# Attention and mixture-of-experts on one core: product 1's base sums are read from PSUM by VectorE, and the next w2's scale comes from a read of its own, a step earlier

## The chip, the cores and the metric

The kernel runs on one core of a Trainium2 chip. The metric is the device time of one execution in microseconds (us). The engines are TensorE (PE in the profile; its weight loads are PEld), VectorE (DVE), ScalarE (ACT), GpSimd (POOL) and SyncE (SP), which here issues nearly all DMA transfers, in one order.

## What is computed

The reference, cut to its core. Attention has 4 batches, 8 heads, 768 positions and 64 numbers a head; its output is the input of a layer with 8 experts, in which every expert works on all 3072 rows:

```python
scores = np.where(mask, scale * np.matmul(q, k.transpose(0, 1, 3, 2)), -1e9)
attn = softmax(scores)
x = np.matmul(attn, v)                      # as 3072 x 512
P = balance(np.exp(x @ w_gate))             # 3072 x 8, eight rounds of normalising
for e in range(8):
    h = np.maximum(x @ w1[e], 0.0)          # 512 -> 1024
    ye = h @ w2[e]                          # 1024 -> 512
    out += P[:, e:e+1] * ye
```

## The kernel before

**Arithmetic.** All numbers are float32 on the outside. For TensorE each operand is scaled by a power of two and split into two float16 parts, and three of the four products of parts are added. The matrix products of the experts are made with seven products instead of eight for each 2 x 2 block of sub-matrices, so there are sums of sub-matrices of x, w1, w2 and h to make (GpSimd, VectorE), scales to find (eight passes of `magnitude`, L122, on ScalarE, then `whole`, `spread` and `power` in `scale_steps`), and splits (`queue_split`: ScalarE writes the high part, L1281, VectorE the low part, L1285).

**Stages.** Attention takes the first 440 us or so. Then 32 steps follow, i = 4e + b for expert e and batch b. The main loop weaves two generators: `outputs(i)`, which calls `stage2` (the second layer: h times w2, 42 units of 12 matmuls at L1801 into banks `py`, each followed by an eviction into `acc` by VectorE, L1823), and `products(i+1)`, which calls `stage1` (the first layer for the next step: for each of four column groups seven products of 12 matmuls at L1664 into banks `p`, with VectorE's `comb`, L1513, then a high part of h on ScalarE, L1680, and a low part on VectorE, L1685 and L1691, or GpSimd, L1691). At the end of a column group `add` makes four sums on GpSimd, `s` (L1750) and three more (L1303); they wait for ScalarE's `a` (L1747), and parts of h wait for them.

**The fine products.** From the third expert on, two of the seven products (0 and 1) are themselves made with seven sub-products of 6 matmuls (L1552). `fine(i+1)` does that, one step ahead, in 14 pieces that `products` puts between the products of `stage1`; the table `BETWEEN` tells how many pieces come after which product of which column group. Product 0 uses the banks fx, fy, fz, product 1 the banks gx, gy, gz. The banks of `p`, f and g are four in all (`ps_h`). The first sub-product of each is a base that is added to what three of the four quarters become. For product 1 this is

```python
nc.scalar.activation(t0, two(bx), AF.Copy, scale=HDOWN)      # L1609, from gx
nc.gpsimd.tensor_tensor(out=at_(sums_, f, t), in0=t0, in1=at_(pair, f, t), op=ALU.add)
```

the second line (L1612) three times; the fourth quarter is made by `comb` from gx after its second sub-product. `xpf` holds the parts of x that the sub-products need; it is loaded again (L1437) for product 1 and for the next step's product 0, after its last reader.

**Weights.** One buffer `r` of 2 MB (tag "r") takes the raw weights in turn: w1 of the next expert is loaded in an expert's second step (`b == LB1`), w2 of the next expert in the last step, after the second of its seven products, both by L205 on SyncE. A buffer with the tag "s3" holds w1's third sum, or w2's first sum `t1`. What has to be done with a weight is not written where it runs but handed to `Slots`: three queues with estimated costs, which `tick` empties as the estimated busy times of VectorE, ScalarE and GpSimd allow. `need(key)` runs all that is left of a key. Work of some keys is also held back to its place by an ordering edge (`not_earlier`). For w2 before the change the order in the queue is: eight passes of the scale, `whole`, `spread` (a TensorE transpose into `all_w`, L135), `power`, then the sums (`queue_sum`, L1296) and splits of `split_w2`. The last scheduling is the compiler's, which orders every engine by its own estimate.

Of the kernel before, what the change touches and what calls it, by code (L numbers as in the profile page):

```python
# [9 lines left out]
F32 = mybir.dt.float32  # L10
# [10 lines left out]
P = 128  # L21
# [35 lines left out]
def tile_sparse_attention_moe(  # L57
# [153 lines left out]
        open_w(which, e)  # L211
        load_part(which, e, 0, 1)

    def scale_steps(which, e, vector=nc.vector, scalar=nc.scalar):
        flat = wr[which].rearrange("p c f -> p (c f)")
        n = 8
        w = KD * FF // n
        m = small.tile([P, n], F32, tag="mxw", name=f"mx_w{which}_{e}")
        a = small.tile([P, 1], F32, tag="maw", name=f"ma_w{which}_{e}")
        s = small.tile([P, 1], F32, tag=f"sw{which}", name=f"sw{which}_{e}")  # L220
        inv = small.tile([P, 1], F32, tag=f"iw{which}", name=f"iw{which}_{e}")
        wr["s", which], wr["i", which, e] = s, inv

        def part(k):
            magnitude(scalar, m[:, k : k + 1], flat[:, k * w : (k + 1) * w])

        def whole():
            vector.tensor_reduce(out=a, in_=m, axis=AX.X, op=ALU.max)

        def spread():  # L230
            wr["all", which] = spread_bound(a, spread_bank[0](f"all_w{which}_{e}"))

        def power():
            vector.tensor_reduce(out=a, in_=wr["all", which], axis=AX.X, op=ALU.max)
            vector.tensor_scalar(a, a, TINY, HUGE, ALU.max, ALU.min)
            ai = a.bitcast(I32)
            vector.tensor_scalar(ai, ai, 0x7F800000, None, ALU.bitwise_and)
# [965 lines left out]
    class Slots:  # L1203
# [13 lines left out]
        def run(self, queue, n):  # L1217
            fn, key, _, costs, _ = queue.pop(n)
            self.charge(costs)
            self.last[id(queue)] = self.now  # L1220
            if key[0] in ("scale", "w1", "w2", "late", "balance", "fine_x"):
                not_earlier(fn)
            else:
                fn()
# [4 lines left out]
                for x, c, lead in zip(self.busy, costs, LEADS)  # L1229
            )  # L1230

        def tick(self, pe, dve, act=0.0, turn=1.0, pool=0.0):
            self.now += turn
            self.pe += pe
            self.busy = [max(x, self.pe - lag) for x, lag in zip(self.busy, LAGS)]
            self.charge((dve, act, pool))
            n, held = 0, set()
            while n < len(self.urgent):
                _, key, ready, costs, _ = self.urgent[n]
                if key not in held and ready <= self.now and self.fits(costs):  # L1240
                    self.run(self.urgent, n)
                    n, held = 0, set()
                    continue
                held.add(key)
                if key[0][0] == "sum":
                    held.update((("h", key[1], p),) + key[1:] for p in (2, 4, 5, 6))
                n += 1
            for queue in (self.lazy, self.calm):
                while queue and self.due(queue):
                    self.run(queue, 0)  # L1250
# [18 lines left out]
    def scale_w(which, e):  # L1269
        parts, whole, spread, power = scale_steps(which, e, Pinned.vector, Pinned.scalar)  # L1270
        key = ("scale", which, e)
        for k, part in enumerate(parts):
            slots.add(part, key, 8 if k == 0 else 1, True, act=0.65)
        slots.add(whole, key, 1, True, dve=0.1)
        slots.add(spread, key, 1, True, gap=5)
        slots.add(power, key, 1, True, dve=0.8, gap=2)

    def queue_split(dst, src, key, delay=1):
        s = wr["s", 1 if key[0] == "w1" else 2]
# [78 lines left out]
    def split_w2(e, r):  # L1358
        h = KF // 2
        m = {  # L1360
            (j, k): r[:, j * h : (j + 1) * h, k * DH : (k + 1) * DH]
            for j in range(2) for k in range(2)
        }
        t1 = raw.tile([P, h, DH], F32, tag="s3", name=f"t1_{e}") if e else wr["t1"]

        def one(p, src):
            queue_split(w2p[p], src, ("w2", e, p))

        def sums():
            if e:  # L1370
                one(1, m[1, 0])
                queue_sum(t1, m[0, 1], m[0, 0], ("scale", 2, e))
                queue_sum(m[0, 1], m[0, 1], m[1, 1], ("scale", 2, e))

        def first():
            if e:
                one(0, m[0, 0])
                queue_sum(m[0, 0], m[1, 1], t1, ("w2", e, 5))
                queue_sum(m[1, 0], m[1, 0], m[0, 0], ("w2", e, 3))

        def second():
            one(6, m[0, 1])
            if e:
                one(5, m[0, 0])

        return [
            sums,
            first,
            second,
            lambda: (one(4, t1), one(3, m[1, 0]), one(2, m[1, 1])),  # L1390
        ]

    def balance():
# [125 lines left out]
    def fine(i, used=None):  # L1519
# [47 lines left out]
        def fresh(nm):  # L1567
            return two(upool.tile([P, TH], F32, tag="u", name=f"{nm}_{i}"))

        def tick(n, m, k=0.0):  # L1570
            slots.tick(0.495, 0.55 * n, 0.5 * m, 0.5, k)

        product = pieces(0)
        bx, t0 = bank_("fx"), fresh("t0")
# [28 lines left out]
        tick(1, 0)  # L1603
        yield

        product1 = pieces(1)
        bx, t0 = bank_("gx"), fresh("s0")
        product1(0, bx, True)
        nc.scalar.activation(t0, two(bx), AF.Copy, scale=HDOWN)  # L1609

        def base(f, t):
            nc.gpsimd.tensor_tensor(  # L1612
                out=at_(sums_, f, t), in0=t0, in1=at_(pair, f, t), op=ALU.add
            )

        base(1, 0)
        base(1, 1)
        tick(0, 1, 1.9)
        yield
        product(2, bz, False)  # L1620
        comb(t5, two(bz), t5)
        last(0)
        base(0, 1)
        tick(1, 0, 0.95)
        yield
        product1(1, bx, False)
        comb(at_(sums_, 0, 0), two(bx), at_(pair, 0, 0))
# [19 lines left out]
        yield  # L1647

    BETWEEN = {
        (1, 4): 1, (1, 2): 1, (2, 5): 1, (2, 6): 1, (2, 3): 1, (2, 4): 2, (2, 2): 2,  # L1650
        (3, 5): 1, (3, 6): 1, (3, 3): 1, (3, 4): 1, (3, 2): 1,
    }

    def stage1(i, qi, used=None):
# [238 lines left out]
    def outputs(i):  # L1893
        e, b = divmod(i, B)
        last = b == B - 1 and e + 1 < NE
        for n, p in enumerate(ORDER2):
            yield from stage2(i, p)
            if p == 4 and e + 1 < NE:
                move_acc(b, 1, True)
            if p == 4 and B <= i + 1 < NI:  # L1900
                move_acc((b + 1) % B, 1, False)
            if last and n == 1:
                for x in range(NP + 2):
                    slots.need(("w1", e + 1, x))
                load_w(2, e + 1)
                parts = split_w2(e + 1, wr[2])
                scale_w(2, e + 1)
                parts[0]()
                queue_weight(e + 1)
            elif last and n in (2, 4, 6):  # L1910
                parts[n // 2]()

    for i in range(NI):
# [8 lines left out]
            for p in range(NP):  # L1922
                slots.need(("w2", e, p))
        if b == LB1 and nxt:
            slots.need(("scale", 2, e + 1))
            load_w(1, e + 1)
            scale_w(1, e + 1)
            sum_w1(e + 1)
# [57 lines left out]
```

## Time and profile before

| | us |
|---|---|
| median of 3 runs | 2186.58 |
| lowest and highest run | 2185.72, 2186.83 |
| the profiled execution | 2186.69 |
| its span | 2184.8 |
| TensorE busy | 2124.3 (97%) |
| VectorE, ScalarE, GpSimd busy | 1662.7 (76%), 1241.0 (57%), 1623.0 (74%) |

The span is what the profiler saw between the first and the last instruction; 1.9 us of the execution lie around it. TensorE is busy for almost all of the span, at the full granted clock in all slices, so the time hangs on the 60.5 us in which it is not, and on whether they grow. In the rows below a bracket at the end of a line gives the idle time of the engine just before it and the instruction that ended it.

### The profile page before, as it was taken

To read this page: it belongs to the slowest core of one execution; us is meant where nothing else is said; L and a number is where in the kernel's file an instruction comes from. 1 tells how busy PE (TensorE), PEld (TensorE's weight loads), DVE (VectorE), ACT (ScalarE), POOL (GpSimd) and SP (SyncE) were. 2 spreads that over 40 slices of the span, in tenths; PEclk is the share of its full clock that TensorE was granted. 3 is DMA by queue.
4 is the path that set the end of the run, shared out by engine and by line. 5 is a ranking of instruction groups with operands and counts; after the bars stand their busy time and mean duration, and the time that the engine had idled before them with its cause. 6 is when DMAs were issued, how large, how long until landed. Compare 5 with 4: busy or idle time off the path is not lost.

```text
span 2184.8 us, 49326 instructions
## 1 busy us (share of the span) xinstructions
PE 2124.3 (97%) x19660; PEld 1644.7 (75%) x19660; DVE 1662.7 (76%) x3082; ACT 1241.0 (57%) x2386; POOL 1623.0 (74%) x1766
## 2 busy tenths in 40 slices
PE   6999999999999999999999999999999999999999
PEld 4777776677777777787878787877787777777787
DVE  8889998778877677767776777677777777777765
ACT  5888888766565556454555454445544555455442
POOL 5667778567668786878687868786878687868763
PEclk9999999999999999999999999999999999999999
DMA  6757795142244434443434343434343434343331
GB/s 171 191 128 172 172 213 142 51 156 102 97 151 162 144 111 162 146 140 117 162 131 155 124 162 124 162 124 162 123 162 124 162 124 162 123 162 131 124 102 66
DMA packets 220986, 305.73 MB, mean 140 GB/s; under 512 B 135228, under 2 KB 153684, under 8 KB 220756
## 3 DMA queue, kind: packets, MB, share of 16 engines
q1 hardware_dynamic: 220192, 302.56, 44.2%
q8 instruction: 153, 2.51, 0.5%
q14 instruction: 77, 0.63, 0.1%
q10 hardware_dynamic: 564, 0.03, 0.0%
HBM read 206.60 MB, written 64.49 MB: 124 GB/s over the span
## 4 chain that ended last, share of the span: by engine, by line
PE 71%; POOL 15%; DVE 7%; ACT 4%; issue 3%; DMA 1%; POOLq 0%; ACTq 0%; DVEq 0%
PE py L1801 31%; PE p L1664 23%; POOL r L1296 3%; POOL h L1691 3%; PE u L837 3%; DVE top L748 2%; POOL s L1750 2%; PE t L772 2%; PE t L775 2%; PE m L739 2%; PE m L742 2%; PE gy L1552 1%; PE fy L1552 1%; POOL r L1303 1%; POOL a L1303 1%
## 5 line engine op out<-in xcount | busy, mean ns | idle before, releaser
L1801 PEld LDWEIGHTS <-h 128*128 128x128 f16 x8064 | 786.1, 98 | 149.1 <-issue 14.3
L1801 PE MATMUL py<-w2p,h 128*128 128x256 f16 x4608 | 578.1, 273 | 8.6 <-DVE acc L1823 7.9
L1801 PE MATMUL py<-vault,h 128*128 128x256 f16 x3456 | 412.5, 273 | 2.9 <-DVE vault L1285 2.9
L1823 DVE SCALAR_TENSOR_TENSOR acc<-py,spare,acc 128x256 f32<-128x256 f32 (+1 forms) x588 | 301.8, 517 | 128.2 <-PE py L1801 120.8
L1750 POOL TENSOR_TENSOR s<-a,u 128x384 f32<-128x384 f32 x128 | 142.4, 1113 | 288.1 <-ACT a L1747 288.1
L1513 DVE SCALAR_TENSOR_TENSOR a<-p,a 128x384 f32<-128x384 f32 x384 | 211.5, 551 | 64.0 <-PE p L1664 62.0
L1691 POOL TENSOR_TENSOR h<-r,h 128x384 f16<-128x384 f32 x224 | 238.3, 1068 | 19.5 <-ACT h L1680 19.5
L1664 PEld LDWEIGHTS <-attic 128*128 128x128 f16 x1824 | 177.2, 98 | 94.0 <-issue 3.3
L1664 PE MATMUL p<-attic 128*128 128x384 f16 x1152 | 217.6, 326 | 0.6 <-DVE h L1685 0.4
L1680 ACT ACTIVATE h<-p 128x384 f16<-128x384 f32 x288 | 139.5, 484 | 136.7 <-DVE p L1513 136.3
L1685 DVE SCALAR_TENSOR_TENSOR h<-p,h 128x384 f16<-128x384 f32 x288 | 159.3, 553 | 62.7 <-ACT h L1680 29.4
L780 ACT ACTIVATE pe<-t,qk 128x768 int32<-128x768 f32 x192 | 172.4, 900 | 58.8 <-PE t L775 46.3
L748 DVE TENSOR_REDUCE top<-m 128x1 f32<-128x768 f32 x192 | 182.0, 950 | 29.8 <-PE m L742 28.7
L1664 PEld LDWEIGHTS <-w1p 128*128 128x128 f16 x1248 | 121.3, 98 | 63.8 <-issue 2.2
L1691 DVE TENSOR_TENSOR h<-s,h 128x384 f16<-128x384 f32 x128 | 106.3, 830 | 78.7 <-ACT h L1680 77.7
L1680 ACT ACTIVATE h<-s 128x384 f16<-128x384 f32 x128 | 66.6, 521 | 174.6 <-POOL s L1750 174.5
L1680 ACT ACTIVATE h<-r 128x384 f16<-128x384 f32 x224 | 114.3, 519 | 90.0 <-POOL r L1303 71.4
L1513 DVE SCALAR_TENSOR_TENSOR p<-p,u 128x384 f32<-128x384 f32 x256 | 142.7, 557 | 25.0 <-PE p L1664 23.4
L794 POOL TENSOR_SCALAR pl<-pe 128x768 f16<-128x768 uint16 x126 | 109.1, 867 | 68.1 <-ACT pe L780 67.4
L1303 POOL TENSOR_TENSOR r<-s,r 128x384 f32<-128x384 f32 x128 | 152.9, 1195 | 7.7
L1664 PEld LDWEIGHTS <-arena 128*128 128x128 f16 x1152 | 112.1, 98 | 61.2 <-issue 2.6
L837 PE MATMUL u<-vq,pl 128*128 128x65 f16 x1152 | 142.5, 193 | 1.0 <-POOL pl L794 0.6
(261 smaller groups left out, 4802.4 us busy)
## 6 DMA issues: line engine op xcount, KB each, us to landing
arena<-xd SPq DMA_DIRECT2D x126, 384.0 KB, 3.6
accd<-acc SPq DMA_DIRECT2D x56, 768.0 KB, 4.8
acc<-accd SPq DMA_DIRECT2D x56, 768.0 KB, 4.8
attic<-xd SPq DMA_DIRECT2D x96, 384.0 KB, 5.2
r<-in_moe_w_dram SPq DMA_DIRECT2D x14, 2048.0 KB, 9.2
xpf<-xfd SPq DMA_DIRECT2D x48, 384.0 KB, 4.9
arena<-in_q_dram SPq DMA_DIRECT2D x16, 384.0 KB, 4.1
arena<-in_k_dram SPq DMA_DIRECT2D x16, 384.0 KB, 4.5
```

The costliest lines, as they stand in the source:

```text
L748: nc.vector.tensor_reduce(out=tops[n][:, c : c + 1], in_=sc[:, :S], axis=AX.X, op=ALU.max)
L780: nc.scalar.activation(pe, sc[:, :S], AF.Exp, bias=EXP_SHIFT, scale=qk[n // 2][3])
L837: nc.tensor.matmul(uv[:, c, :n], lhsT=l[:, c * P : (c + 1) * P], rhs=w[:, h, kc, :n], start=(kc == 0 and c == 0 and m == 0), stop=(kc == N ...
L1303: nc.gpsimd.tensor_tensor(out=out, in0=x, in1=y, op=ALU.subtract)
L1513: nc.vector.scalar_tensor_tensor(out=t, in0=ps, scalar=HDOWN, in1=other, op0=ALU.mult, op1=ALU.add)
L1664: nc.tensor.matmul(ps, lhsT=w1ps[i // B][p][:, l, kc, fs], rhs=xp[p][:, r, kc], start=(kc == 0 and m == 0), stop=(kc == KH - 1 and m == 2),)
L1680: nc.scalar.activation(h[:, 0], src, AF.Relu if relu else AF.Copy)
L1685: nc.vector.scalar_tensor_tensor(out=h[:, 1], in0=src, scalar=0.0, in1=h[:, 0], op0=ALU.max, op1=ALU.subtract,)
L1691: eng.tensor_tensor(out=h[:, 1], in0=src, in1=h[:, 0], op=ALU.subtract)
L1750: nc.gpsimd.tensor_tensor(out=s1, in0=a1, in1=u3, op=ALU.add)
L1801: nc.tensor.matmul(py, lhsT=hs[i, p, kc][:, l, tsl], rhs=w2p[p][:, r, kc], start=(old is None and kc == 0 and m == 0), stop=(kc == KF // 2 ...
L1823: nc.vector.scalar_tensor_tensor(out=dst, in0=src, scalar=c, in1=dst, op0=ALU.mult, op1=ALU.add)
```

## The change

Two edits. In `fine`, the base of product 1 is no longer copied by ScalarE and added by GpSimd: VectorE makes the three base sums itself, each a `comb` with gx in PSUM as one operand. The piece that holds product 0's last sub-product now comes ahead of the piece with product 1's first, and `BETWEEN` puts one piece less after the sixth product of the third column group and one more after the first product of the fourth. `tick` loses its argument for GpSimd.

In the other, w2's scale is no longer taken from the 2 MB load itself. `early_scale(e+1)`, queued behind the last splits of w2 of expert e, that is in the first steps of expert e, fetches w2 of the next expert in four parts of 512 KB into a buffer of the tag "s3" and runs the eight passes on them, then `whole`, `spread` and `power`. All of it must be done before w1 of the next expert is loaded. When w2 is loaded for good, its sums and splits are queued without a scale ahead of them, under keys of their own, and the first split has a delay of 10.

```diff
+    def early_scale(e):
+        key = ("early", e)
+        steps = []
+
+        def fetch(k):
+            if k == 0:
+                t = raw.tile([P, KH, FH], F32, tag="s3", name=f"w2_{e}")
+                flat = t.rearrange("p k f -> p (k f)")
+                steps.extend(scale_steps(2, e, Pinned.vector, Pinned.scalar, flat))
+                steps.append(flat.rearrange("p (k f) -> p k f", f=DM))
+            nc.sync.dma_start(
+                out=steps[4],
+                in_=w2[e].rearrange("(c p) f -> p c f", p=P)[:, 2 * k : 2 * k + 2],
+            )
+
+        for k in range(KF // 2):
+            slots.add(lambda k=k: fetch(k), key, 1, True)
+            for n in range(2):
+                slots.add(
+                    lambda k=2 * k + n: steps[0][k](), key, 1, True, act=0.65,
+                    gap=0 if n else 5,
+                )
+        for n, (gap, dve) in enumerate(((0, 0.1), (5, 0.0), (2, 0.8))):
+            slots.add(lambda n=n: steps[1 + n](), key, 1, True, dve=dve, gap=gap)
...
         def sums():
             if e:
-                one(1, m[1, 0])
-                queue_sum(t1, m[0, 1], m[0, 0], ("scale", 2, e))
-                queue_sum(m[0, 1], m[0, 1], m[1, 1], ("scale", 2, e))
+                one(1, m[1, 0], 10)
+                queue_sum(t1, m[0, 1], m[0, 0], ("w2", e, 4))
+                queue_sum(m[0, 1], m[0, 1], m[1, 1], ("w2", e, 6))
...
+        def last():
+            one(4, t1)
+            one(3, m[1, 0])
+            one(2, m[1, 1])
+            if e + 1 < NE:
+                early_scale(e + 1)
...
-        product1 = pieces(1)
-        bx, t0 = bank_("gx"), fresh("s0")
-        product1(0, bx, True)
-        nc.scalar.activation(t0, two(bx), AF.Copy, scale=HDOWN)
-
-        def base(f, t):
-            nc.gpsimd.tensor_tensor(
-                out=at_(sums_, f, t), in0=t0, in1=at_(pair, f, t), op=ALU.add
-            )
-
-        base(1, 0)
-        base(1, 1)
-        tick(0, 1, 1.9)
-        yield
         product(2, bz, False)
         comb(t5, two(bz), t5)
         last(0)
-        base(0, 1)
-        tick(1, 0, 0.95)
+        tick(1, 0)
+        yield
+
+        product1 = pieces(1)
+        bx = bank_("gx")
+        product1(0, bx, True)
+        for f, t in (0, 1), (1, 1), (1, 0):
+            comb(at_(sums_, f, t), two(bx), at_(pair, f, t))
+        tick(3, 0)
         yield
...
-        (1, 4): 1, (1, 2): 1, (2, 5): 1, (2, 6): 1, (2, 3): 1, (2, 4): 2, (2, 2): 2,
-        (3, 5): 1, (3, 6): 1, (3, 3): 1, (3, 4): 1, (3, 2): 1,
+        (1, 4): 1, (1, 2): 1, (2, 5): 1, (2, 6): 1, (2, 3): 1, (2, 4): 1, (2, 2): 2,
+        (3, 5): 2, (3, 6): 1, (3, 3): 1, (3, 4): 1, (3, 2): 1,
...
                 load_w(2, e + 1)
                 parts = split_w2(e + 1, wr[2])
-                scale_w(2, e + 1)
                 parts[0]()
...
         if b == LB1 and nxt:
-            slots.need(("scale", 2, e + 1))
+            slots.need(("early", e + 1))
             load_w(1, e + 1)
```

## Rows read from the trace of the kernel before

**Rows 1.** Busy us (x instructions) by stretch, then granted PE clock, DMA share, GB/s.
```profile
0.00:440.00 440.00, 412.76 (x5501) 294.92 (x5502) 383.68 (x674) 349.96 (x508) 301.83 (x452) 1.00 0.64 156
...
1244.00:1466.00 222.00, 217.25 (x1830) 173.51 (x1828) 162.88 (x306) 112.02 (x236) 176.02 (x173) 1.00 0.41 141
```

**Rows 2.** What PE waits for, whole span: us in total, times, longest us.
```profile
PE py L1801 <- DVE acc L1823: 7.9, 6, 1.3
...
PE fx L1552 <- ACT t L1576: 7.0, 11, 1.2
...
PE p L1664 <- DVE h L1685: 5.7, 7, 1.0
...
PE py L1801 <- DVE vault L1285: 2.9, 6, 0.5
...
PE fy L1552 <- DVE a L1513: 2.2, 5, 0.4
...
PE all_w L135 <- DVE ma_w L228: 1.8, 2, 1.1
```

**Rows 3.** Timeline of PE, 1344 to 1363 us: start, duration, line, instruction, [idle before].
```profile
1348.27 3.76 PE L1801 MATMUL py<-vault,h 128*128 128x256 f16 x33 [0.47 <-DVE vault L1285]
...
1353.19 0.49 PE L1552 MATMUL fx<-arena,w1p 128*128 128x192 f16 x4 [0.18 <-ACT t L1576]
...
1362.16 0.71 PE L1801 MATMUL py<-w2p,h 128*128 128x256 f16 x5 [1.33 <-DVE acc L1823]
```

**Rows 4.** Timeline of PE, ACT and POOL, 1229 to 1256 us, the turn's D to F.
```profile
1230.21 1.27 POOL L1296 TENSOR_TENSOR r<-r 128x512 f32<-128x512 f32 x1
...
1234.43 4.55 POOL L1296 TENSOR_TENSOR r<-r 128x512 f32<-128x512 f32 x2
...
1239.99 0.53 ACT L1680 ACTIVATE h<-s 128x384 f16<-128x384 f32 x1 [3.41 <-POOL s L1750]
...
1240.42 1.14 ACT L1281 ACTIVATE arena<-r,sw 128x1024 f16<-128x1024 f32 x1
...
1246.12 1.14 PE L1664 MATMUL p<-arena,attic 128*128 128x384 f16 x6 [1.01 <-DVE h L1685]
...
1248.77 0.66 PE L1552 MATMUL fx<-arena,w1p 128*128 128x192 f16 x6 [1.18 <-ACT t L1576]
...
1254.51 0.66 PE L1552 MATMUL fy<-xpf,w1f 128*128 128x192 f16 x6 [0.45 <-DVE a L1513]
```

**Rows 5.** Timeline of POOL, ACT and DVE, 1339 to 1363 us, the turn's A to C.
```profile
1341.81 3.78 POOL L1296 TENSOR_TENSOR r<-r,t 128x256 f32<-128x256 f32 x4
...
1346.42 4.05 POOL L1296 TENSOR_TENSOR r<-r 128x256 f32<-128x256 f32 x3
...
1351.48 0.52 ACT L1680 ACTIVATE h<-s 128x384 f16<-128x384 f32 x1 [4.71 <-POOL s L1750]
...
1356.82 1.13 ACT L1281 ACTIVATE w2p<-r,sw 128x1024 f16<-128x1024 f32 x1
...
1360.54 0.90 DVE L1691 TENSOR_TENSOR h<-s,h 128x384 f16<-128x384 f32 x1 [3.02 <-ACT h L1680]
```

**Rows 6.** What SyncE's queue waits for; and us to landing of L1437's reload near 1370.
```profile
SPq L205 <- DVE w2p L1285: 190.7, 7, 32.7
...
DMA to landing us min/median/max: 4.5/4.5/4.5
```

**Rows 7.** Groups of instructions by form: count | busy us, mean ns | idle before, releaser.
```profile
L1612 POOL TENSOR_TENSOR r<-s,a 128x384 f32<-128x384 f32 x72 | 77.7, 1093 | 59.6 <-ACT s L1609 32.1 <-ACT a L1747 16.2 <-DVE h L1685 6.1
...
L1513 DVE SCALAR_TENSOR_TENSOR a<-p,a 128x384 f32<-128x384 f32 x384 | 211.5, 551 | 64.0 <-PE p L1664 62.0
...
L1691 DVE TENSOR_TENSOR h<-s,h 128x384 f16<-128x384 f32 x128 | 106.3, 830 | 78.7 <-ACT h L1680 77.7
```

**Rows 8.** Busy us of PE, PEld, DVE, ACT, POOL in 8 us behind two gx.
```profile
1315.90:1323.90 8.00, 8.00 (x68) 6.08 (x66) 6.17 (x14) 3.20 (x6) 7.10 (x7) 1.00 0.61 218
...
1370.90:1378.90 8.00, 8.00 (x71) 6.37 (x69) 5.22 (x12) 2.11 (x5) 5.30 (x6) 1.00 0.79 282
```

More of the change, by code (lines that the diff above doesn't have):

```diff
@@ L212, in load_w, with scale_steps @@
         load_part(which, e, 0, 1)
-    def scale_steps(which, e, vector=nc.vector, scalar=nc.scalar):
-        flat = wr[which].rearrange("p c f -> p (c f)")
+    def scale_steps(which, e, vector=nc.vector, scalar=nc.scalar, flat=None):
+        flat = wr[which].rearrange("p c f -> p (c f)") if flat is None else flat
         n = 8
@@ L224, in part @@
         def part(k):
-            magnitude(scalar, m[:, k : k + 1], flat[:, k * w : (k + 1) * w])
+            at_ = k * w % flat.shape[1]
+            magnitude(scalar, m[:, k : k + 1], flat[:, at_ : at_ + w])
         def whole():
@@ L1220, in run @@
             self.last[id(queue)] = self.now
-            if key[0] in ("scale", "w1", "w2", "late", "balance", "fine_x"):
+            if key[0] in ("early", "scale", "w1", "w2", "late", "balance", "fine_x"):
                 not_earlier(fn)
@@ L1230, in fits, with tick @@
             )
-        def tick(self, pe, dve, act=0.0, turn=1.0, pool=0.0):
+        def tick(self, pe, dve, act=0.0, turn=1.0):
             self.now += turn
@@ L1235, in tick @@
             self.busy = [max(x, self.pe - lag) for x, lag in zip(self.busy, LAGS)]
-            self.charge((dve, act, pool))
+            self.charge((dve, act, 0.0))
             n, held = 0, set()
@@ L1364, in split_w2, with one @@
         t1 = raw.tile([P, h, DH], F32, tag="s3", name=f"t1_{e}") if e else wr["t1"]
-        def one(p, src):
-            queue_split(w2p[p], src, ("w2", e, p))
+        def one(p, src, delay=1):
+            queue_split(w2p[p], src, ("w2", e, p), delay)
         def sums():
             if e:
-                one(1, m[1, 0])
-                queue_sum(t1, m[0, 1], m[0, 0], ("scale", 2, e))
-                queue_sum(m[0, 1], m[0, 1], m[1, 1], ("scale", 2, e))
+                one(1, m[1, 0], 10)
+                queue_sum(t1, m[0, 1], m[0, 0], ("w2", e, 4))
+                queue_sum(m[0, 1], m[0, 1], m[1, 1], ("w2", e, 6))
         def first():
@@ L1389, in split_w2 @@
             second,
-            lambda: (one(4, t1), one(3, m[1, 0]), one(2, m[1, 1])),
+            last,
         ]
@@ L1568, in fresh, with tick @@
             return two(upool.tile([P, TH], F32, tag="u", name=f"{nm}_{i}"))
-        def tick(n, m, k=0.0):
-            slots.tick(0.495, 0.55 * n, 0.5 * m, 0.5, k)
+        def tick(n, m):
+            slots.tick(0.495, 0.55 * n, 0.5 * m, 0.5)
         product = pieces(0)
```

## The prediction, made before the changed kernel had run

> **What bounds the kernel now.** Three views were read in this order. First the table by stretches: attention leaves TensorE 440.00 − 412.76 = 27.2 us idle, which the change does not touch; an expert's turn of 222 us leaves 222.00 − 217.25 = 4.75, with the clock at full [rows 1]. No TensorE work is added or removed, so the change can only win idle TensorE time in the expert part, or make more of it. Second, the list of what TensorE waits for [rows 2], without the attention's own. Third, the timeline of one turn, which shows that these totals are six short gaps that come back every turn at the same places: A 0.47, B 0.18, C 1.33 [rows 3], and, 102 us ahead of A, D 1.01, E 1.18, F 0.45 [rows 4]. A repeats 6 times (2.9), C 6 times (7.9), F 5 times (2.2) [rows 2]. The fx row (7.0, 11 times) holds B and E: B is 6 × 0.18 = 1.1 and E the other 5.9. Of the 5.7 before `p`, D is 5 × 1.01 = 5.0. The scale's transpose `all_w` adds 1.8. Together 2.9 + 1.1 + 7.9 + 5.0 + 5.9 + 2.2 + 1.8 = 26.8 us: **all that can be won**, so no time below 2186.7 − 26.8 = 2159.9 is reasoned for.
>
> Where A, B and C come from: GpSimd makes the sums of the new w2 (L1296) only after the scale, at the pace of the queue, and they run in one row, 3.78 us for four and 4.05 for three, just when the batch's own sum `s` (L1750) wants the engine. ScalarE stands 4.71 us until `s` is there [rows 5]; the vault's split (A) and the copy of fx (B) are late. A split of w2, 1.13 us, is then ahead of the next `s` on ScalarE, VectorE stands 3.02 us for what follows it, and the eviction queued behind is C [rows 5]. D, E and F are the same with w1: two sums take 4.55 us ahead of `s`, ScalarE is idle 3.41, and the split on VectorE (D), the copy of fx (E) and the combination out of fy's bank (F) are late [rows 4].
>
> **The early scale.** Removed: the scale of w2 from its own load. Added, in the step before: four fetches of 512 KB (7 × 2 MB in all), the same eight ScalarE passes as before, no new arithmetic. The sums and splits of w2 no longer wait for a scale; they can start as the load lands, at the pace of the planner's queue. The order shows it on GpSimd ahead of the first `s` of batch 17 (expert 4's second batch; `r_4` and `t_4` are the raw w2 and its first sum). Before:
>
> ```order
> L1303 TENSOR_TENSOR c_16_3_19775<-c_16_3_19775,r_16_1_18914 128x384
> L1296 TENSOR_TENSOR r_4_19318<-r_4_19318 128x256 x2
> L1691 TENSOR_TENSOR h_8134<-r_16_1_18914,h_8134 128x384
> L1296 TENSOR_TENSOR r_4_19318<-r_4_19318,t_4_19320 128x256 x4
> L1691 TENSOR_TENSOR h_8127<-c_16_3_19775,h_8127 128x384
> L1296 TENSOR_TENSOR r_4_19318<-r_4_19318 128x256 x3
> L1750 TENSOR_TENSOR s_17_0_20071<-a_17_0_19501,u_17_0_19974 128x384
> ```
>
> The same place on GpSimd with the change:
>
> ```order
> L1329 TENSOR_TENSOR c_16_3_19792<-c_16_3_19792,r_16_1_18939 128x384
> L1717 TENSOR_TENSOR h_8130<-r_17_0_19519,h_8130 128x384
> L1322 TENSOR_TENSOR r_4_19341<-r_4_19341 128x256
> L1717 TENSOR_TENSOR h_8134<-r_16_1_18939,h_8134 128x384
> L1717 TENSOR_TENSOR h_8125<-r_17_0_19519,h_8125 128x384
> L1717 TENSOR_TENSOR h_8127<-c_16_3_19792,h_8127 128x384
> L1322 TENSOR_TENSOR r_4_19341<-r_4_19341 128x256
> L1776 TENSOR_TENSOR s_17_0_20073<-a_17_0_19518,u_17_0_19982 128x384
> ```
>
> Nine sums have become two; the rest stand earlier. The seven measured ones took 3.78 + 4.05 = 7.8 us [rows 5], more than the 4.71 that ScalarE lost; nor has ScalarE's order a split right ahead of the next `s`'s input any more. A, B and C go: **−11.9**. `all_w` now follows its passes by a queue's distance in a step where nothing waits for it: **−1.8**. The eight passes only move, on a ScalarE that is busy 112 of 222 us [rows 1]: nothing. On SyncE the w1 load waits for the last w2 split, up to 32.7 us now [rows 6]; that split comes earlier, so the two fetches queued around the load cost it nothing.
>
> **The base sums.** Removed, 24 times: one ScalarE copy of gx and three GpSimd adds with mean 1.09 us [rows 7]. Added, 24 times: three VectorE combinations that read gx from PSUM, of a kind that takes 0.55 us [rows 7]. gx's bank is also held for three reads instead of one, and its second product waits for the third read. On VectorE, in batch 17's last steps (`gx` is product 1's first bank, `fz` the last of product 0). Before:
>
> ```order
> L1513 SCALAR_TENSOR_TENSOR a_17_1_19611<-p_17_2_20370,a_17_1_19611 128x384
> L1513 SCALAR_TENSOR_TENSOR a_18_0_20222<-fz_20350,a_18_0_20222 128x2x192
> L1513 SCALAR_TENSOR_TENSOR r_18_0_20223<-gx_20359,a_18_0_20222 128x2x192
> L1513 SCALAR_TENSOR_TENSOR a_17_1_19611<-p_17_3_20419,a_17_1_19611 128x384
> L1823 SCALAR_TENSOR_TENSOR acc_8153<-py_4_2_20462,spare_19897,acc_8153 128x256
> ```
>
> With the change:
>
> ```order
> L1546 SCALAR_TENSOR_TENSOR a_18_0_20229<-fz_20362,a_18_0_20229 128x2x192
> L1546 SCALAR_TENSOR_TENSOR r_18_0_20230<-gx_20408,a_18_0_20229 128x2x192
> L1546 SCALAR_TENSOR_TENSOR r_18_1_20339<-gx_20408,a_18_1_20338 128x2x192 x2
> L1717 TENSOR_TENSOR h_8145<-s_17_2_20380,h_8145 128x384
> L1546 SCALAR_TENSOR_TENSOR a_17_1_19627<-p_17_3_20423,a_17_1_19627 128x384
> ```
>
> Three reads of gx now stand in a row ahead of a subtraction and of the combination that lets TensorE's bank `p` go; the fourth read comes seven entries later. Their price is bounded by 0 (all in VectorE's idle time) and 24 × 3 × 0.55 = 39.6 us (all of it on TensorE's path). In the 8 us behind gx VectorE is busy 5.2 to 6.2 [rows 8], so it has 1.8 to 2.8 to spare for 3 × 0.55 = 1.65: it catches up, but what is queued behind the three is late for a moment. The nearest row for such a lateness is F, 0.45 us of TensorE behind one late combination [rows 4]; I take it in every second step, 12 × 0.45 = **+5.4**.
>
> The Trainium skill (VectorE: DVE Perf Modes, Rules for kernel authors) speaks against this edit: for elementwise work on a matmul's output take the slow PSUM rate, or copy to SBUF first where there are many operations. The rows do not bear it out here: with a PSUM operand 551 ns, the two-SBUF-operand subtraction of the same size 830 [rows 7]; by the page, the old copy would be the cheaper form for VectorE.
>
> GpSimd gets back 3.3 us a step. For D to F this shows in the order only in part. GpSimd ahead of batch 15's first `s`, before (`r_4` is here the raw w1):
>
> ```order
> L1296 TENSOR_TENSOR r_4_17773<-r_4_17773 128x512
> L1321 TENSOR_TENSOR s_4_17779<-r_4_17773 128x256 x2
> L1321 TENSOR_TENSOR s_4_17779<-s_4_17779,r_4_17773 128x256
> L1321 TENSOR_TENSOR s_4_17779<-r_4_17773,s_4_17779 128x256
> L1296 TENSOR_TENSOR r_4_17773<-r_4_17773 128x512 x2
> L1750 TENSOR_TENSOR s_15_0_18655<-a_15_0_18103,u_15_0_18562 128x384
> ```
>
> With the change:
>
> ```order
> L1717 TENSOR_TENSOR h_8144<-c_14_3_18396,h_8144 128x384
> L1347 TENSOR_TENSOR s_4_17806<-r_4_17800 128x256 x2
> L1347 TENSOR_TENSOR s_4_17806<-s_4_17806,r_4_17800 128x256
> L1347 TENSOR_TENSOR s_4_17806<-r_4_17800,s_4_17806 128x256
> L1322 TENSOR_TENSOR r_4_17800<-r_4_17800 128x512 x2
> L1776 TENSOR_TENSOR s_15_0_18682<-a_15_0_18130,u_15_0_18590 128x384
> ```
>
> One 512-wide sum of 1.27 us [rows 4] has left the row; the 4.55 us pair is still there. `s` comes 1.27 earlier, enough for D's 1.01 and F's 0.45: **−5.0 and −2.2**. TensorE then reaches E 1.01 sooner, so E would still be 1.18 + 1.01 − 1.27 = 0.92, unless ScalarE's split of 1.14 at 1240.42 [rows 4], which the change puts ahead of `s`, falls into its idle 3.41. Between 0 and 0.92 I take half of E: **−3.0**.
>
> **Sum**, against the profiled run's 2186.7 (span 2184.8 and 1.9 around it; the median is 0.1 lower): −11.9 − 1.8 − 5.0 − 2.2 − 3.0 = −23.9, and +5.4: −18.5, **2168 us**, with 2161 to 2173 for other shares of the new waits.
>
> **Rivals.** (1) *Half*: A to C and `all_w` go (−13.7), D to F stay, since the 4.55 us pair still stands ahead of `s`; with few new waits 2173 to 2178. For it: 1.27 us is just over D's 1.01. (2) *It does not do what it says*: w2's splits are bound by the load itself and the sums pile up as before; 2186. Against it: the new order, seven sums earlier. (3) *Slower, through VectorE*: the three reads find a queue already behind. Sub-product 2 of gx comes some 4 us of TensorE work after the first (my estimate from the order and the matmuls' lengths); with over 4 − 1.65 = 2.35 us of backlog TensorE waits for the bank, and evictions and splits behind come up to 1.65 late. If every step pays in full: 2186.7 − 23.9 + 39.6 = 2202.4. It beats the gain from 1.0 us a step on (23.9 / 24). For it: VectorE is the engine named in five of the six rows of waits [rows 2]. Against it: the spare 1.8 us. (4) *The reload of xpf*: it lands 4.5 us after its issue where a weight load runs beside it [rows 6], and the order leaves it 5 to 6 us of TensorE work (an estimate, again from the order). Held on SyncE behind a fetch that waits for two passes it could be 1 to 4 us late, 24 times at worst: 2186.7 − 18.5 + 24 × 1 = 2192. Against it: the fetches' passes stand earlier in ScalarE's order than xpf's last readers in TensorE's.
>
> **How the numbers follow.** Forecast 0.60; half 0.18; no effect 0.07; VectorE 0.08; xpf 0.04; 0.03 for a time below 2161. The range takes the forecast, its low end all 26.8 with no new wait, the half and a part of the cases between half and nothing: 2159 to 2183, about 0.81. A change of 0.2% (4.4 us) is about what a measurement of this kernel can tell from none. Faster: 0.60 + 0.18 + 0.03 = 0.81, less 0.02 for a half eaten up by waits = 0.79; slower 0.08 + 0.03 = 0.11; same 0.10.
>
> **What would show it.** In the profile after: the rows of waits for `vault`, `acc` and `all_w` gone; the one of `p` on the split and of fy small; fx at most 3 us. GpSimd idle ahead of `s` of each batch 4e+1. New rows "gx or gy or py waits for VectorE a, r or acc" of some 5 us together. Wrong if A to C are still there, if the waits on VectorE are over 15 us, or if `xpf` by DMA appears.

## The result, and the profile after

| | before | changed |
|---|---|---|
| median, us | 2186.7 | 2164.7 |
| ratio, 95% interval | | 0.9892 [0.9878, 0.9906] |
| profiled execution, span, us | 2184.8 | 2162.5 |
| TensorE, VectorE busy, us | 2124.3, 1662.7 | 2124.2, 1706.8 |
| ScalarE, GpSimd busy, us | 1241.0, 1623.0 | 1237.6, 1524.3 |

The change makes the kernel 1.1% faster, 22 us. One of the four runs of the changed kernel took 3164.6 us at a mean granted clock of 0.66, and is in the median but not in the ratio; the other three took 2162.5 to 2165.2. The same kernel in two later sets of runs gave 2160.3 and 2162.9 beside a kernel before of 2186.7 and 2187.2, so the gain is 22 to 26 us. The forecast was 2168, with a range of 2159 to 2183.

The table by stretches of the changed kernel (columns as in [rows 1]) shows where the gain lies: in a stretch of 220 us of an expert's turn TensorE is now idle 0.11 us, where a turn of 222 us had 4.75 [rows 1]. Attention's 440 us have 27.9 us of idle, where they had 27.2.

```profile
0.00:440.00 440.00, 412.06 (x5485) 293.99 (x5486) 379.41 (x671) 348.30 (x503) 300.93 (x450) 1.00 0.64 156
...
800.00:1020.00 220.00, 217.18 (x1816) 173.08 (x1815) 173.06 (x320) 116.01 (x239) 159.37 (x162) 0.99 0.46 153
...
1240.00:1460.00 220.00, 219.89 (x1857) 176.13 (x1855) 172.35 (x322) 113.55 (x237) 161.32 (x165) 1.00 0.45 152
```

What TensorE waits for, whole span (us in total, times, longest), without attention's own. Of the six rows of [rows 2] the ones of `acc`, fx and `vault` are gone, with all six gaps A to F; what stands for `p`, fy and `cs` are single events, the next view.

```profile
PE cs L1451 <- DVE spare L1445: 2.9, 3, 1.8
PE p L1690 <- DVE h L1711: 2.7, 2, 2.2
...
PE all_w L135 <- DVE ma_w L229: 0.6, 2, 0.4
PE fy L1585 <- ACT a L1614: 0.6, 1, 0.6
```

The timeline of TensorE in the changed kernel, its gaps from 640 us on (start, duration, instruction, idle before and releaser): three single losses that the kernel before did not have, 1.81 us at 647 and 0.56 and 2.24 at 809 to 814, and then no gap but a scale's 0.41 to the end.

```profile
646.98 0.39 PE L1451 MATMUL cs<-spare,ones 128*128 128x8 f32 x2 [1.81 <-DVE spare L1445]
771.38 0.23 PE L135 MATMUL all_w<-ident_b,ma_w 128*128 128x128 bf16 x1 [0.15 <-DVE ma_w L229]
809.22 0.66 PE L1585 MATMUL fy<-xpf,w1f 128*128 128x192 f16 x6 [0.56 <-ACT a L1614]
814.41 0.97 PE L1690 MATMUL p<-attic,arena 128*128 128x384 f16 x5 [2.24 <-DVE h L1711]
1815.43 0.23 PE L135 MATMUL all_w<-ident_b,ma_w 128*128 128x128 bf16 x1 [0.41 <-DVE ma_w L229]
```

At the place of A to C the row of sums ahead of `s` is gone. Before, three sums of 4.05 us in all stood right there [rows 5]; now one of 0.73 is left, and GpSimd then waits 2.96 us for the operand of `s`:

```profile
1338.87 0.73 POOL L1322 TENSOR_TENSOR r<-r 128x256 f32<-128x256 f32 x1
1342.56 1.12 POOL L1776 TENSOR_TENSOR s<-a,u 128x384 f32<-128x384 f32 x1 [2.96 <-ACT a L1773]
```

### The profile page after: what moved, and what is told of

Its sections match the earlier page's. It is cut to its first block, busy times and chain, and to the rows that moved or that the text cites. A ratio compares the mean times of both kernels' runs of the same rounds, so it can differ in the third digit from the quotient of the medians.

```text
span 2162.5 us, 49389 instructions
## 1 busy us (share of the span) xinstructions
PE 2124.2 (98%) x19660; PEld 1646.8 (76%) x19660; DVE 1706.8 (79%) x3154; ACT 1237.6 (57%) x2362; POOL 1524.3 (70%) x1694
## 4 chain that ended last, share of the span: by engine, by line
PE 80%; DVE 8%; POOL 6%; ACT 3%; issue 2%; DMA 1%; POOLq 0%; ACTq 0%; DVEq 0%
PE py L1827 35%; PE p L1690 27%; PE u L838 3%; PE t L773 2%; PE t L776 2%; PE m L740 2%; PE m L743 2%; DVE top L749 2%; PE fy L1585 1%; PE gy L1585 1%; PE fx L1585 1%; PE gz L1585 1%; PE fz L1585 1%; PE gx L1585 1%; POOL s L1776 1%
## 5 line engine op out<-in xcount | busy, mean ns | idle before, releaser
L1827 PE MATMUL py<-w2p,h 128*128 128x256 f16 x4608 | 587.1, 273 | 0.0
L1717 POOL TENSOR_TENSOR h<-r,h 128x384 f16<-128x384 f32 x224 | 228.4, 1027 | 18.2 <-ACT h L1706 17.5
L1717 DVE TENSOR_TENSOR h<-s,h 128x384 f16<-128x384 f32 x128 | 114.1, 892 | 51.2 <-ACT h L1706 50.5
L1768 ACT ACTIVATE u<-p 128x384 f32<-128x384 f32 x128 | 62.7, 490 | 151.8 <-DVE p L1546 151.2
```

The source lines that it names most:

```text
L1717: eng.tensor_tensor(out=h[:, 1], in0=src, in1=h[:, 0], op=ALU.subtract)
L1827: nc.tensor.matmul(py, lhsT=hs[i, p, kc][:, l, tsl], rhs=w2p[p][:, r, kc], start=(old is None and kc == 0 and m == 0), stop=(kc == KF // 2 ...
```

## The experiments

### One part of the change at a time

The early scale alone: the fine products as before, with the old order of pieces, `BETWEEN` and charges.

```diff
         product1 = pieces(1)
-        bx = bank_("gx")
+        bx, t0 = bank_("gx"), fresh("s0")
         product1(0, bx, True)
-        for f, t in (0, 1), (1, 1), (1, 0):
-            comb(at_(sums_, f, t), two(bx), at_(pair, f, t))
-        tick(3, 0)
+        nc.scalar.activation(t0, two(bx), AF.Copy, scale=HDOWN)
...
+        base(1, 0)
+        base(1, 1)
+        tick(0, 1, 1.9)
...
```

> Only the early scale of w2; the base of product 1 is copied by ScalarE and added by GpSimd as before, with the old order of the pieces. Theory (gaps A to C and the scale's transpose belong to w2's scale, D to F to GpSimd's base adds): A, B, C and all_w gone, 13.7 us, D to F still there: 2186.7 - 13.7 = 2173. Rival 1 (D to F come from the late weights too, and the early scale, which lets w1 be loaded earlier, removes them by itself): all gone, about 2162 to 2165. Rival 2 (the early scale needs the room that the base adds leave on GpSimd): A to C stay in part, 2180 or more.

Measured 2175.6, ratio 0.9946 [0.9931, 0.9961], −11.6. The gaps of its TensorE timeline, in one turn:

```profile
1245.68 1.14 PE L1697 MATMUL p<-arena,attic 128*128 128x384 f16 x6 [1.11 <-DVE h L1718]
1248.33 0.66 PE L1585 MATMUL fx<-arena,w1p 128*128 128x192 f16 x6 [1.19 <-ACT t L1609]
1254.07 0.66 PE L1585 MATMUL fy<-xpf,w1f 128*128 128x192 f16 x6 [0.45 <-DVE a L1546]
```

D, E and F stand there as they did [rows 4], and A, B and C are gone. The saving is 2 us short of the expected 13.7, and this kernel has the new single gaps too, 4.6 us of them (0.56 at 806.68, 2.25 at 811.87, 1.8 before `cs`); the next kernel, without the early scale, has none of the three, so they come with the early scale. Both rivals fall: w1's earlier load does not remove D to F, and the early scale needs no room from the other part.

The base sums alone, w2's scale from its own load (an edit against the kernel before):

```diff
-        bx, t0 = bank_("gx"), fresh("s0")
-        product1(0, bx, True)
-        nc.scalar.activation(t0, two(bx), AF.Copy, scale=HDOWN)
+        bx = bank_("gx")
+        product1(0, bx, True)
+        for f, t in (0, 1), (1, 1), (1, 0):
+            comb(at_(sums_, f, t), two(bx), at_(pair, f, t))
...
```

> Only the base sums on VectorE, with the new order of the pieces; w2's scale from its own load as before. Theory: D, E and F gone, 13.1 us, A to C and all_w there as before: 2186.7 - 13.1 = 2173.6. Rival 1 of the run with the early scale alone: nothing but a little, 2184 to 2187. If the two parts add up, the savings of the two runs sum to 22.

Measured 2176.8, ratio 0.9950 [0.9935, 0.9965], −10.3, where 2173.6 was expected. D to F are gone, but A to C are not "as before". One gap stands in their place, the same in each turn:

```profile
1348.61 0.66 PE L1552 MATMUL fx<-arena,w1p 128*128 128x192 f16 x6 [2.56 <-ACT t L1576]
```

Where A, B and C cost 0.47 + 0.18 + 1.33 = 1.98 [rows 3], this is 2.56. In this kernel's timeline of ScalarE three splits of w2 (1.15, 1.15 and 1.14 us) stand between 1341.2 and 1344.9, and then ScalarE waits for GpSimd until 1346.89, so that the copy of fx comes at 1348.06. The late scale still has to be paid for at that place, only elsewhere in it. The savings of the two runs, 11.6 + 10.3 = 21.9, add up to the low end of the whole, 22 to 26.

### Is it GpSimd's work, or the planner's account of it?

D to F were laid to GpSimd's work. So three adds of the same size, to a tile that nobody reads, were put back on it, with the planner told of them:

```diff
+        s0 = fresh("s0")
+
+        def idle_add(f, t):
+            nc.gpsimd.tensor_tensor(
+                out=s0, in0=at_(pair, f, t), in1=at_(pair, f, t), op=ALU.add
+            )
+
+        idle_add(1, 0)
+        idle_add(1, 1)
-        tick(3, 0)
+        tick(3, 0, 1.9)
...
+        idle_add(0, 1)
-        tick(1, 0)
+        tick(1, 0, 0.95)
```

> The changed kernel with GpSimd's work put back: three adds of the same size at the place of the old base adds, written to a tile that nobody reads, with the planner told of them as before; VectorE still makes the base sums. Theory (GpSimd's three adds are what made D to F): the waits before fx on ScalarE's t, before p on VectorE's h and before fy come back, up to 13 us, 2165 + 5 to 13 = 2170 to 2178. Rival (D to F went because of the new order of the pieces and of ScalarE's work): no change, 2163 to 2166.

Measured 2184.7, ratio 0.9988 [0.9979, 0.9998]: +20 us over the changed kernel, nearly the whole gain. The gaps of a turn:

```profile
1172.30 0.23 PE L135 MATMUL all_w<-ident_b,ma_w 128*128 128x128 bf16 x1 [1.62 <-DVE ma_w L229]
1248.08 1.14 PE L1700 MATMUL p<-arena,attic 128*128 128x384 f16 x6 [0.38 <-DVE h L1721]
1250.72 0.66 PE L1585 MATMUL fx<-arena,w1p 128*128 128x192 f16 x6 [1.19 <-ACT t L1609]
1256.47 0.66 PE L1585 MATMUL fy<-xpf,w1f 128*128 128x192 f16 x6 [0.44 <-DVE a L1546]
```

E and F are back in full, D with a third of its 1.01, and a gap before the scale's transpose, 9.0 us in 6 times, is new. That looked like the theory's win, though the time is 7 us above its range. The kernel keeps the new order of the pieces and has no copy of gx, so neither of these alone keeps the gaps away. But two things had changed, GpSimd's work and the planner's account, and the next run parts them: the same adds, with `tick(3, 0)` and `tick(1, 0)`.

> The kernel with the three idle GpSimd adds put back (2184.7), now without telling the planner of them: its queues are paced as in the changed kernel. Theory (the adds themselves take the time on GpSimd that makes D, E and F late): D to F are back, 5 x 2.0 = 10 us over the changed kernel, 2171 to 2176; the 9.0 us before the scale's transpose were the planner's charge and are gone. Rival (it was the planner's charge that moved all of it): 2160 to 2166.

Measured 2165.2, beside 2162.9 for the changed kernel (a third set of it, below). GpSimd is busy 1578.8 us, 55 more than in the changed kernel, and the gaps D to F do not come back. What is left is the wait before the scale's transpose:

```profile
PE all_w L135 <- DVE ma_w L229: 5.8, 6, 2.0
```

So for D to F the theory fell and its rival stands: **the account moved them, not the work**. The timeline of GpSimd ahead of the `s` behind which D lies (L1786 here), first of the kernel that tells:

```profile
1231.37 0.91 POOL L1727 TENSOR_TENSOR h<-c,h 128x384 f16<-128x384 f32 x1
1232.24 1.27 POOL L1322 TENSOR_TENSOR r<-r 128x512 f32<-128x512 f32 x1
...
1236.47 3.49 POOL L1322 TENSOR_TENSOR r<-r 128x512 f32<-128x512 f32 x2
1239.92 1.99 POOL L1786 TENSOR_TENSOR s<-a,u 128x384 f32<-128x384 f32 x1
```

and of the one that does not:

```profile
1223.72 0.92 POOL L1727 TENSOR_TENSOR h<-c,h 128x384 f16<-128x384 f32 x1
1224.59 1.42 POOL L1347 TENSOR_TENSOR s<-r 128x256 f32<-128x256 f32 x2
...
1227.60 3.47 POOL L1322 TENSOR_TENSOR r<-r 128x512 f32<-128x512 f32 x2
1233.26 1.01 POOL L1786 TENSOR_TENSOR s<-a,u 128x384 f32<-128x384 f32 x1 [2.19 <-ACT a L1783]
```

The second has no 512-wide sum of its own between `h<-c,h` and L1347. This is the sum of 1.27 us [rows 4] that the prediction saw leave the row. With 2.85 us a step charged to GpSimd, the planner holds the weight sums back; without, it lets them go earlier. The adds' own time is not free: the 5.8 us before `all_w` stand against 0.3 in the changed kernel of the same set, so most of the 9.0 comes without the account, against what this theory said. The medians are only 2.3 us apart, and the profiled executions differ in the clock as well: it fell twice in the changed kernel's, for some 1.7 us each, and not once in this one's.

### How much room VectorE has

Each base sum made three times over:

```diff
-        for f, t in (0, 1), (1, 1), (1, 0):
+        for f, t in ((0, 1), (1, 1), (1, 0)) * 3:
```

> The changed kernel with each of the three base sums made three times over (six more reads of gx by VectorE in each of 24 steps, 24 x 6 x 0.55 = 79 us of VectorE more, the result the same). Theory (the three reads lie in VectorE's idle time, TensorE has banks in store, and only a part of nine will not): 2165 + 0 to 30. Rival (VectorE is close to the bound behind gx): the spare 1.8 to 2.8 us less 1.65 leaves 0.2 to 1.2 for 3.3 us more, so 2.1 to 3.1 us a step, 24 x = 50 to 74 us, 2215 to 2239.

Measured 2169.0, ratio 0.9918 [0.9903, 0.9933]: 4 to 9 us over the three sets of the changed kernel, for 144 instructions more of 0.55 us, 79 us if added up (VectorE's busy time rises by 1750.9 − 1706.8 = 44: in the record one starts before the last has ended, three take 1.49, and some other operations took less, the 128 subtractions at L1717 107.5 us in all instead of 114.1). What TensorE waits for on their account is the row of gy, and a copy of fx late by 0.45 in a turn:

```profile
PE gy L1585 <- DVE r L1546: 3.4, 5, 1.5
...
1247.65 0.66 PE L1585 MATMUL fx<-arena,w1p 128*128 128x192 f16 x6 [0.45 <-ACT t L1609]
```

Nine reads cost a few us; three cost nothing that shows. The idle 1.8 to 2.8 us of [rows 8] are no measure of the limit, since the nine also spread out between other work. The first three and the last of them in one step of this kernel:

```profile
1261.45 1.49 DVE L1546 SCALAR_TENSOR_TENSOR r<-gx,a 128x384 f32<-128x384 f32 x3
...
1269.06 0.54 DVE L1546 SCALAR_TENSOR_TENSOR r<-gx,a 128x384 f32<-128x384 f32 x1
```

### Reading PSUM against a copy in SBUF

ScalarE copies gx to SBUF as before the change, and VectorE adds from there:

```diff
+        nc.scalar.activation(t0, two(bx), AF.Copy, scale=HDOWN)
         for f, t in (0, 1), (1, 1), (1, 0):
-            comb(at_(sums_, f, t), two(bx), at_(pair, f, t))
+            nc.vector.tensor_tensor(
+                out=at_(sums_, f, t), in0=t0, in1=at_(pair, f, t), op=ALU.add
+            )
-        tick(3, 0)
+        tick(3, 1)
```

> The changed kernel with gx copied to SBUF by ScalarE first, as before the change, and the three sums made by VectorE from SBUF operands alone (tensor_tensor). Theory (three reads of PSUM at 0.55 us each are no dearer than SBUF adds, 0.83 by the row of the subtraction): VectorE busy up by 24 x 3 x 0.28 = 20 us, most of it hidden, 2164 to 2170. Rival (by the rule to copy out of PSUM where there are several operations): VectorE busy down, the adds under 0.55 us, 2160 to 2165.

Measured 2190.1, ratio 1.0016 [1.0006, 1.0025]: the whole gain is lost, and both expectations were far off. The instruction groups of VectorE, the adds of this kernel and the reads of gx of the changed one (count | busy us, mean ns | idle before), and the row of TensorE's waits that is new:

```profile
L1650 DVE TENSOR_TENSOR r<-s,a 128x384 f32<-128x384 f32 x72 | 89.3, 1292 | 8.1 <-ACT s L1648 7.5
...
PE p L1693 <- DVE a L1546: 20.8, 22, 1.8
```
```profile
L1546 DVE SCALAR_TENSOR_TENSOR r<-gx,a 128x384 f32<-128x384 f32 x96 | 48.7, 549 | 2.9 <-DVE a L1546 0.5
```

An add of two SBUF operands takes 1292 ns in the mean, one PSUM operand 549. VectorE is busy 1752.6 us in all, about as in the run with nine reads (1750.9), yet this one costs some 21 us more: the three adds follow each other without anything between, and behind them waits the combination that lets bank `p` go. ScalarE's copy and the half microsecond that the planner is told of for it came along; no run parts them from the adds, but the 20.8 us of the new row are waits on VectorE. GpSimd's instructions of the same stretch are shown too.

```profile
1271.66 1.19 POOL L1329 TENSOR_TENSOR r<-s,r 128x384 f32<-128x384 f32 x1
1271.92 3.81 DVE L1650 TENSOR_TENSOR r<-s,a 128x384 f32<-128x384 f32 x3
...
1272.82 1.23 POOL L1720 TENSOR_TENSOR h<-a,h 128x384 f16<-128x384 f32 x1
...
1274.01 1.30 POOL L1329 TENSOR_TENSOR c<-c,r 128x384 f32<-128x384 f32 x1
...
1275.65 0.55 DVE L1546 SCALAR_TENSOR_TENSOR a<-p,a 128x384 f32<-128x384 f32 x1
...
1276.25 1.14 PE L1693 MATMUL p<-attic 128*128 128x384 f16 x6 [1.81 <-DVE a L1546]
```

A busy share says little: behind an uninterrupted block of 3.8 us TensorE waits in spite of its four banks (22 times, up to 1.8 us), where nine reads with other work between them cost a few us. Whether it is the instruction or its operands was tried with the instruction of the changed kernel on the SBUF copy:

```diff
-            nc.vector.tensor_tensor(
-                out=at_(sums_, f, t), in0=t0, in1=at_(pair, f, t), op=ALU.add
-            )
+            nc.vector.scalar_tensor_tensor(
+                out=at_(sums_, f, t), in0=t0, scalar=1.0, in1=at_(pair, f, t),
+                op0=ALU.mult, op1=ALU.add,
+            )
```

> The base sums from ScalarE's copy in SBUF (2190.1) with the instruction that reads PSUM in the changed kernel, scalar_tensor_tensor, in the place of tensor_tensor. Theory (two operands in SBUF make the adds long beside a busy GpSimd, whatever the instruction): mean over 1.0 us, 2180 to 2192. Rival (it is the instruction): mean about 0.55 us, 2160 to 2168.

Measured 2190.5, ratio 1.0017 [1.0007, 1.0026], with the adds as long:

```profile
L1650 DVE SCALAR_TENSOR_TENSOR r<-s,a x72: 558/1346/1569, 821.6 to 2097.6; 128x384 f32<-128x384 f32 x72
```

(shortest, median, longest in ns). It is the operands. The record also shows what the adds wait for. In these two kernels 140 of the 144 adds start while an instruction of GpSimd is running, and each of them ends 0.41 to 0.42 us behind the end of that instruction; above, the third one ends at 1275.73 and GpSimd's at 1275.31. The other four start in a break between two instructions of GpSimd and take 0.56. In the changed kernel a read of gx takes 0.54 to 0.56, whatever GpSimd does. The Trainium skill (SBUF — State Buffer, SBUF: two separate sides) names a cause: VectorE with two SBUF inputs and GpSimd use one pair of ports, and who comes second is blocked for the whole instruction. The trace agrees, by the 140 and the 4.

### The order of the pieces

The three reads at the old place, ahead of product 0's last sub-product:

```diff
-        product(2, bz, False)
-        comb(t5, two(bz), t5)
-        last(0)
...
         product1(0, bx, True)
         for f, t in (0, 1), (1, 1), (1, 0):
             comb(at_(sums_, f, t), two(bx), at_(pair, f, t))
+        product(2, bz, False)
+        comb(t5, two(bz), t5)
+        last(0)
...
+        (1, 4): 1, (1, 2): 1, (2, 5): 1, (2, 6): 1, (2, 3): 1, (2, 4): 2, (2, 2): 2,
+        (3, 5): 1, (3, 6): 1, (3, 3): 1, (3, 4): 1, (3, 2): 1,
```

> The changed kernel with the old order of the pieces and the old places between the products: product 1's first sub-product, with its three reads by VectorE, ahead of product 0's last. Theory (TensorE has enough in store either way): 2163 to 2168. Rival (the new order is what hides the three reads, since by the order gx's second product now comes 1 us of TensorE work later than before): 0.4 to 1.2 us in each of 24 steps, 2174 to 2193.

Measured 2161.3, beside 2160.3 for the changed kernel. In this form the third sum is made before its operand has its last term, so the kernel leaves that term out of one quarter; the work of all engines is the same. The form that takes it in moves one of the three reads a piece later:

```diff
-        for f, t in (0, 1), (1, 1), (1, 0):
+        for f, t in (1, 0), (1, 1):
             comb(at_(sums_, f, t), two(bx), at_(pair, f, t))
-        tick(3, 0)
+        tick(2, 0)
         yield
         product(2, bz, False)
         comb(t5, two(bz), t5)
         last(0)
-        tick(1, 0)
+        comb(at_(sums_, 0, 1), two(bx), at_(pair, 0, 1))
+        tick(2, 0)
```

> The old order of the pieces and the old places once more, now with the third base sum behind product 0's last term, which it needs: two reads of gx after its first sub-product and one in the next piece. Theory (the order of the pieces is not what hides the reads): 2160 to 2166, as the changed kernel. Rival (it is): 0.4 to 1.2 us in each of 24 steps, 2170 to 2190.

Measured 2158.2, ratio 0.9867 [0.9852, 0.9882], where the changed kernel beside it had 2162.9: the fastest time of the study, against the expectation of no difference. How much of it is the order? The transposes `all_w` of expert 2's w1, first of the changed kernel in this set, then of this one:

```profile
769.58 0.23 PE L135 MATMUL all_w<-ident_b,ma_w 128*128 128x128 bf16 x1 [0.28 <-DVE ma_w L229]
```
```profile
766.94 0.23 PE L135 MATMUL all_w<-ident_b,ma_w 128*128 128x128 bf16 x1 [0.27 <-DVE ma_w L229]
```

2.6 of the spans' 4.5 us (2160.0 and 2155.5) are there at 767 us, ahead of any fine product, so the order of the pieces has not made them by itself. 2.4 of them are there at the end of attention, where the two kernels do the same (the first matmul into `p` is at 405.52 and 403.09), and there, from 330 to 350 us, the granted clock was 0.91 in the one execution and 1.00 in the other. The 1.9 behind are small against the spread of the changed kernel's own three sets (2160.3 to 2164.7). The new order of pieces is then neither needed to hide the reads nor shown to harm.

### The one gap that the change brings

At 809 to 814 us TensorE waits 2.8 us at the first fine products. The passes of expert 2's w1 start at 757.72 in the changed kernel, and at 741.36 before, and its last sums are late: GpSimd makes two of them, 2.50 us, right ahead of `s`, and ScalarE waits 2.49 us for `s`, as in D.

```profile
757.72 0.63 ACT L122 ACTIVATE unread<-r 128x512 bf16<-128x512 f32 x1
...
807.57 2.50 POOL L1322 TENSOR_TENSOR r<-r 128x512 f32<-128x512 f32 x2
...
810.03 1.98 POOL L1776 TENSOR_TENSOR s<-a,u 128x384 f32<-128x384 f32 x1
...
812.04 0.52 ACT L1706 ACTIVATE h<-s 128x384 f16<-128x384 f32 x1 [2.49 <-POOL s L1776]
```

Two kernels ran beside each other: the changed one, and one with expert 2's early passes closer together in the queue.

```diff
-                    gap=0 if n else 5,
+                    gap=0 if n else (2 if e == 2 else 5),
```

> The changed kernel itself once more, beside the three that follow: 2162 to 2166 again, and in its trace the idle 2.8 us near 809 to 814 us with the granted clock low right behind it.

> The changed kernel with one number changed: the passes of the early scale of expert 2's w2 stand 2 ticks apart in the queue instead of 5. Theory (the one gap that the change brings, 2.8 us at 809 to 814 and the granted clock of 0.66 in the 5 us behind it, comes from expert 2's w1: its scale, queued behind the early passes and the parts of x, starts 16 us later than before, so that its last split is late for the first fine products): the gap and the low clock go, 2164.7 - 2.8 - 1.7 = 2160. Rival (the gap belongs to VectorE's or GpSimd's row there, whatever the scale does): no change, 2163 to 2166.

Measured 2160.3 for the changed kernel, below the 2162 to 2166 expected, and 2163.0 for the other. The passes do start at 747.97, and the 2.24 us gap is gone, but others stand in its place:

```profile
708.48 0.23 PE L135 MATMUL all_w<-ident_b,ma_w 128*128 128x128 bf16 x1 [1.44 <-DVE ma_w L229]
750.99 1.14 PE L1690 MATMUL p<-arena,w1p 128*128 128x384 f16 x6 [1.19 <-DVE h L1711]
763.87 0.23 PE L135 MATMUL all_w<-ident_b,ma_w 128*128 128x128 bf16 x1 [1.51 <-DVE ma_w L229]
801.75 1.14 PE L1690 MATMUL p<-attic,arena 128*128 128x384 f16 x6 [1.02 <-DVE h L1711]
```

Together 5.2 us: the queue's pace was changed, and the side work met TensorE at other places. That w1's late scale makes the gap fits this run, which moved the pace of all side work and not the scale alone; that a smaller number mends the time is not borne out.

> The changed kernel a third time, as the measure for the three that follow: 2160 to 2166, as its two runs so far.

Measured 2162.9 for this third set of the changed kernel.

## Why the prediction was right

The direction and the size held: 2164.7 lies 3.3 us from the 2168 named. That it lies so near is in part luck: E brought 2.9 us more than taken and the three reads cost 5.4 less, while 4.6 us of new gaps were not in the sum. Of the steps, one had the right sum and the wrong reason, and one term was mis-sized. Of the signs named, GpSimd idle ahead of `s` came (2.96 us), the new waits on VectorE a, r or acc did not, and `all_w` went only in part.

- **A to C and `all_w`, −11.9 and −1.8.** All three gaps are gone, and stay gone with the early scale alone, which lacks the other edit. Of the `all_w` 1.8 us, 0.6 are left in other places.
- **D and F, −5.0 and −2.2.** Gone, with the base edit alone. The step named the sum that leaves the row, and it was that sum. The reason it gave, that GpSimd "gets back 3.3 us a step", failed: with that time put back and the planner not told, the gaps stay away. The 4.55 us pair, which the step left as it was, takes 3.48 in the changed kernel and 3.49 in the one that tells, which may be why D came back there at a third.
- **E, −3.0.** All of its 5.9 went, 2.9 more than taken. The split which the order puts ahead of `s` did fall into ScalarE's idle time; half of it was a guess between two ends.
- **The three reads, +5.4.** This term was mis-sized: no wait on them shows in the changed kernel, and six reads more of the same kind cost 4 to 9 us. The step took F, a late combination in a row of other lateness, as the price of an ordinary one. The bound from above, 39.6, was no help: four banks and the py banks lie between a late read and TensorE.
- **What the sum did not have.** The 2.8 us at 809 to 814 and the 1.8 before `cs`, both once in the run, in the steps from attention's end to the first fine products, where the early scale comes into a queue that other work shares. The prediction looked at a turn that repeats and multiplied it; it did not walk through the first turn.

By terms: −11.9 − 1.2 − 5.0 − 2.2 − 5.9 = −26.2 gone in the steady turns, +2.8 + 1.8 new, so −21.6, where the profiled spans differ by 22.3. Two more things are in the difference, and nearly cancel: three dips of the clock, 1.7 us each (below), and a cost of each gap that its idle time does not show. The next instruction of TensorE normally starts before the last has ended. Before the change:

```profile
1240.85 1.47 PE L1801 MATMUL py<-w2p,h 128*128 128x256 f16 x12
1242.16 0.66 PE L1552 MATMUL fx<-arena,w1p 128*128 128x192 f16 x6
...
1243.63 1.47 PE L1801 MATMUL py<-w2p,h 128*128 128x256 f16 x12
```

Twelve matmuls are followed after 1.31 us where nothing waits, and after 2.49 where D lies (1246.12 [rows 4]). D is listed with 1.01 of idle time, and costs 1.18. Some 30 gaps fewer, at 0.16 or 0.17 each, are about 5 us (an estimate from this place). That is why TensorE's busy time is the same in both kernels in spite of the dips, and why the 26.8 us were not all that could be won: the old order of the pieces, with the new gaps still in it, won 29.0 (2187.2 − 2158.2).

The rivals: *half* did not come, because the lost sum's 1.27 us was enough; it needed only the 1.0 of D. *VectorE* fell by the run with nine reads. *xpf* fell: no wait on its DMA is listed, and its landing has the median 3.6 us after, where it was 4.9. The Trainium skill's rule to copy out of PSUM, weighed in the prediction (VectorE: DVE Perf Modes, Rules for kernel authors), speaks against the change, and the two SBUF runs show the reverse, by 28 to 30 us against the changed kernel beside them.

## What to carry to other kernels

Where a planner places side work by accounts of busy time, a moved operation acts through its account as much as through its time: run the operation with the planner told of it and not told, before laying a gain to the engine that it left. Price three operations more on an engine by whether they make one uninterrupted block that outlasts the buffers of whoever waits, and not by their busy time; two kernels here with the same VectorE time lie 21 us apart. Look at where both operands lie: beside a busy GpSimd, two in SBUF took 1.3 us here and one in PSUM 0.55. And walk through the first turn of a loop apart from the one that repeats.

## What was not expected of the hardware

After some of the single gaps of 1.8 to 2.6 us the granted clock of TensorE falls, and after the same gap in another execution it does not. The table by stretches, first of the changed kernel, then of its second set, behind the 2.24 us gap at 814 and 812 us (the granted clock is the third number from the end):

```profile
815.00:820.00 5.00, 5.00 (x29) 3.35 (x27) 3.03 (x7) 1.40 (x3) 2.92 (x4) 0.66 0.00 0
```
```profile
815.00:820.00 5.00, 5.00 (x45) 4.00 (x44) 3.94 (x9) 1.75 (x4) 1.07 (x2) 1.00 0.25 76
```

A mean of 0.66 over 5 us is 1.7 us lost to 1.2 GHz, the lower level, in the place of 2.4: 12 matmuls took 2.76 us there and 1.47 in the other execution. In tables of 10 us the changed kernel has such stretches near 340, 650 and 815, its second set only near 340, and its busy time of TensorE is 2124.2 there and 2120.8 here: 3.4 us, which is two such stretches and more than the 2.5 us between the two spans (2162.5 and 2160.0). The profiled execution of the kernel before had none. The second surprise is the SBUF add: 1.3 us for what one PSUM operand does in 0.55.
